# Transformer block on one core: SyncE's first 24 loads paced, and gate_m computed with the other modulation rows on TensorE

## Chip, core and metric

One core of one Trainium2 chip. The time is the device time in microseconds (us) of one execution. Engines: TensorE (PE; its weight loads are PEld), VectorE (DVE), ScalarE (ACT), GpSimd (POOL), and SyncE (SP), which only issues DMAs here.

## What is computed

A diffusion transformer block with adaptive modulation. B = 2, N = 256 tokens, D = 1152, two heads of 576, F = 4608, all inputs bf16.

```python
mod = (_silu(c) @ w_mod).reshape(B, 6, 1, D)
shift_a, scale_a, gate_a, shift_m, scale_m, gate_m = [mod[:, i] for i in range(6)]
h = _layernorm(x) * (1 + scale_a) + shift_a
q, k, v = split(h @ wqkv)
attn = _softmax(q @ k.T * Dh ** -0.5)
x = x + gate_a * ((attn @ v) @ wo)
h2 = _layernorm(x) * (1 + scale_m) + shift_m
return x + gate_m * (_gelu(h2 @ w_fc1) @ w_fc2)
```

The modulation vectors come from a product of two rows (one for each batch) with a 1152 x 6912 weight, so each of the six takes a 2.65 MB weight for two rows of result.

## The kernel before

**Tiling.** All 512 tokens are worked on at once. D is cut into 9 slices of 128 (`kt`), F into 36 (`f`, `j`). All weights pass once through one SBUF arena of 212,000 bytes per partition, whose regions (O_A, O_B, O_C, O_R, O_X and others) are used again by later stages. A reuse makes a DMA or an operation wait for the last reader.

**Stages on TensorE, in order.** Warm-up matmuls; transposes of the normalized x (`xn_T`); scale_a from three loads of w_mod for the first five slices (`mod_kt(WSC...)`, two columns per matmul); the K projection, slice by slice (`k_pair`), with the rest of scale_a in between; shift_a; the Q projection; scores and softmax; the V projection (`v_proj`), with the transposes of the softmax in between; after `v_proj(2, 0)` the modulation rows (`rows`); after `v_proj(3, 0)` their transposition into columns (`rows_T`); attention times V; the Wo projection (`wo_tile`) with gate_a, residual and second layernorm; fc1 with gelu; fc2 with gate_m, residual and store.

**The modulation rows.** `rows` (L964) computes gate_a, shift_m and scale_m as rows: the stationary operand is the two columns of silu(c) for a slice (`ST[:, kt:18:9]`), the moving one a piece of w_mod, and four matmuls lie side by side in the four 32-column groups of the array (`tile_position=(0, 32 * j)`). Pieces are 448 columns wide (`RW`), two for each group, so the 3456 columns take 18 groups of four over the nine slices, in PSUM banks 3 and 4. One ScalarE and one VectorE copy evict them to ROWS. GpSimd stores gate_a's row to a DRAM scratch and reads it back broadcast over all partitions (`gate_load(0, GA)`); the Wo stage multiplies by it at L1062. `rows_T` (L984) turns shift_m and scale_m into columns with 18 small matmuls.

**gate_m.** It is not among the rows. Its weight (WGM) is loaded by a DMA of its own after the V projection. `gate_m_sums` (L994) computes on VectorE, during fc1, the product by f32 multiply-adds: for each batch nine passes over 128 x 1152 (L1001 and L1004), with silu(c) as a scalar for each partition. Two 32x32 block transposes (L1008) and a reduction (L1010) fold the partitions in each block; `gate_m_rows` (L1012) sums over the four blocks with one small fp32 matmul on TensorE (GMS with QS), and goes over the same DRAM scratch to GM. ST32 and QS are prepared near the start (L726, L728).

**Loads.** SyncE issues all loads, in the order of the code: x in two halves; scale_a weights for the first five slices (three loads of 480 KB); K weights of slices 0 to 4 (288 KB each); the rest of scale_a (three of 384 KB); K weights of slices 5 to 8; shift_a (three of 864 KB); Q weights by slice; V; three of WMODR (2592 KB each); Wo; fc1 weights 0 to 3; WGM; fc2 weights; and further fc1 weights as their buffers come free. Up to shift_a no load waits for anything. The Q weights wait for TensorE to be done with the first matrix in that region.

**What sets the order.** `Sched` collects every operation with its reads and writes and works out dependences (`_track`). TensorE and SyncE keep the order of the code; VectorE and ScalarE follow a hand-written list at the start (`S.first`), and otherwise a list planner that uses estimated durations and the longest path behind each operation (`schedule`). `emit` turns dependences into semaphore waits. An explicit order puts gate_m's multiply-adds behind the eviction of the last `h2T` slices (L1186 to L1190).

Of the kernel before, what the change touches and what calls it, by code (L numbers as in the profile page):

```python
# [516 lines left out]
def c_mm(n):  # L517
    return max(n / 2.4 + 2.5, 27.0)
# [26 lines left out]
def build_kernel(nc, x, c, wqkv, wo, w_mod, w_fc1, w_fc2, out):  # L545
# [5 lines left out]
    with (  # L551
# [46 lines left out]
        WV = wmat(O_C, D)  # L598
        WMODR = wmat(O_R, 3 * D)
        WGM = wmat(O_R + 3 * W1, D)  # L600
        GMT = sb(O_R + 3 * W1, 9216, F32)
        WFC2 = sb(O_R, 4 * W1).rearrange("p (k f) -> p k f", k=JT)
# [14 lines left out]
        GM = [sb(o + 18432, 2304) for o in (O_A, O_C)]  # L617
        XN2 = [sb(O_R + 3 * W1 - (i + 1) * 2304, 2304) for i in range(4)]
        ROWS = sb(O_R + 3 * W1 - 5 * 2304, 1792)
        GMA = sb(O_X, 9216, F32)  # L620
        T1 = [sb(O_X + i * 1536, 1536, F32) for i in range(3)]
# [25 lines left out]
        NHALF = sb(misc(4), 4, F32)  # L647
        ST32 = sb(misc(72), 72, F32)
        GMS = sb(misc(288), 288, F32)
        QS = sb(misc(128), 128, F32)  # L650
        GMO = sb(misc(64), 64)
        MX = sb(misc(32), 32, F32).rearrange("p (i j) -> p i j", i=4)
# [27 lines left out]
        def copy_on(eng, dst, src, n, psum16, name):  # L680
            if eng == "act":
                act(c_act(n), lambda e: e.activation(out=dst, in_=src, func=ACTF.Copy), [src], [dst], name)  # L682
            else:
                dve(c_dve_psum16(n) if psum16 else c_dve_psum32(n), lambda e: e.tensor_copy(dst, src), [src], [dst], name)  # L684

        def mm(o, l, r, st, sp, **kw):
            S.instr(lambda e: e.matmul(o, lhsT=l, rhs=r, start=st, stop=sp, **kw), reads=[l, r], writes=[o])  # L687
# [36 lines left out]
        dve(170, lambda e: e.tensor_scalar(out=HC, in0=CT_PS, scalar1=0.5, scalar2=None, op0=ALU.mult), [CT_PS], [HC], "c_half")  # L724
        i3 = IDENT.rearrange("p (a i) -> p i a", a=4)
        dve(200, lambda e: e.tensor_reduce(out=QS, in_=i3, axis=AX.X, op=ALU.add), [IDENT], [QS], "qs")  # L726
        dve(170, lambda e: e.scalar_tensor_tensor(out=ST, in0=TH, scalar=1.0, in1=HC, op0=ALU.add, op1=ALU.mult), [TH, HC], [ST], "c_silu")
        dve(100, lambda e: e.tensor_copy(ST32, ST), [ST], [ST32], "st32")  # L728

# [231 lines left out]

        RW = 448
# [21 lines left out]
        def rows_T():  # L984
            S.unit("pe", 2 * KT * 27.0, "rowsT")
            for i in range(2 * KT):
                j, o = (KT + i) // 7, (KT + i) % 7
                mm(ps32(5, i * 2, 2), ROWS[0:98, o * 128:(o + 1) * 128], IDENT[0:98, 32 * j:32 * j + 2], i == 0, i == 2 * KT - 1,
                   skip_group_check=True)
            a, b_ = ps32(5, 0, 18), ps32(5, 18, 18)  # L990
# [3 lines left out]
        def gate_m_sums():  # L994
            wfc2_load(2)
            for b in range(2):
                acc = GMA[:, b * D:(b + 1) * D]
                for kt in range(KT):
                    w, s = WGM[:, kt, :], ST32[:, b * KT + kt:b * KT + kt + 1]
                    if kt == 0:  # L1000
                        dve(760, lambda e, w=w, s=s, acc=acc: e.tensor_scalar(out=acc, in0=w, scalar1=s, scalar2=None, op0=ALU.mult),  # L1001
                            [w, s], [acc], "gm_%d_%d" % (b, kt))
                    else:
                        dve(1270, lambda e, w=w, s=s, acc=acc: e.scalar_tensor_tensor(out=acc, in0=w, scalar=s, in1=acc, op0=ALU.mult, op1=ALU.add),  # L1004
                            [w, s, acc], [acc], "gm_%d_%d" % (b, kt))
            for b in range(2):
                acc, t = GMA[:, b * D:(b + 1) * D], GMT[:, b * D:(b + 1) * D]
                dve(1270, lambda e, acc=acc, t=t: e.transpose(t, acc), [acc], [t], "gm_tr%d" % b)  # L1008
            t, o = GMT.rearrange("p (c i) -> p c i", i=32), GMS
            dve(2500, lambda e: e.tensor_reduce(out=o, in_=t, axis=AX.X, op=ALU.add), [t], [o], "gm_sum")  # L1010

        def gate_m_rows():  # L1012
            S.unit("pe", 120.0, "gm_T")
            p = ps32(6, 0, 32)[0:72, :]
            mm(p, GMS, QS, True, True)
            dve(160, lambda e: e.tensor_copy(GMO[0:72, :], p), [p], [GMO[0:72, :]], "gm_ev")  # L1016
            dma(scratch[1].rearrange("b (c i) -> (b c) i", i=32), GMO[0:72, :], 2 * D * 2, "st_gm", eng="pool")
            gate_load(1, GM)

# [134 lines left out]
        for f in range(F0 - 2, F0):  # L1154
            fc1_tile(f, 0, 256)
        gate_m_sums()
        for f in range(F0):
            fc1_tile(f, 256, 256)
        for f in range(F0, JT):
            if f % 4 == 0 and f // 4 >= 4:  # L1160
                wfc1_load(f // 4)
            if f == 30:
                gate_m_rows()
            if f == 32:
                wfc2_load(3)
            fc1_tile(f, 0, 512)
# [18 lines left out]

        by = {u.name: u for u in S.units}  # L1186
        for u in S.units:
            if u.eng == "dve" and u.name.startswith("h2T_3"):
                S.order_after(by["gm_0_0"], u)
        S.order_after(by["gm_1_0"], by["gm_0_8"])  # L1190
        S.schedule()
# [52 lines left out]
```

## Time and profile before

| | |
|---|---|
| Median of 3 runs (lowest, highest) | 248.41 us (247.8, 248.61) |
| Profiled execution: time, span | 247.8 us, 246.1 us |
| TensorE busy | 240.2 us (98%) |
| VectorE busy | 99.2 us (40%) |
| ScalarE, GpSimd busy | 63.8 us, 20.2 us |
| Moved by DMA | 51.59 MB, mean 210 GB/s |
| Modulation weights for rows (L668, three loads of 2592 KB): issued, time to landing | 33.4, 35.0, 35.7 us; 15.2, 19.9, 26.9 us |
| Multiply-adds of gate_m (L1004) | 16 of 1416 ns, from 111.1 to 136.2 us |

How to read it: the span runs from the first to the last instruction of the program, and the time has 1.7 us around it. Busy times overlap between engines. A line number is that of the kernel before. Matmuls are issued before the one ahead has ended, so the time that one matmul costs in a row of them is the distance between starts, not its own duration. DMAs are shown by their issue and the time to their landing; the issuing instruction can be long over by then.

### The profile page before, as it was taken

The numbers are of one execution on the slowest core, as the hardware profiler recorded it, in microseconds if no ns is written. First come the engines' busy times: TensorE is split into PE (matmuls) and PEld (weight loads), VectorE is DVE, ScalarE is ACT, GpSimd is POOL, SyncE is SP. The second block draws the span as 40 slices with busy tenths as digits, with TensorE's granted clock in tenths as the row PEclk, the third lists the DMA queues.
The fourth block names the chain that finished last, engine by engine and source line by source line (L and its number), as shares of the span: only waits on it lengthen the run. The fifth ranks groups of instructions, "written<-read, shape, count | busy, mean of one in ns | idle before, by whom it ended". The sixth has DMA issues, their size and how long they took to land.

```text
span 246.1 us, 4095 instructions
## 1 busy us (share of the span) xinstructions
PE 240.2 (98%) x1789; PEld 149.3 (61%) x1789; DVE 99.2 (40%) x202; ACT 63.8 (26%) x129; POOL 20.2 (8%) x34
## 2 busy tenths in 40 slices
PE   6899999999999999999999999999999999999995
PEld 2589954557666766798544444444566666666675
DVE  2843440456312679969999700000011222211112
ACT  4830340344311405984322223322000000000000
POOL 1300000000011166500000000020000000000000
PEclk9999999999999999999999999999999999999999
DMA  6999989999993999969943579011000000000000
GB/s 232 362 377 392 390 307 410 420 421 409 389 349 91 332 381 392 390 228 394 352 121 131 189 246 377 3 30 67 0 19 16 16 19 17 16 16 19 24 24 19
DMA packets 28844, 51.59 MB, mean 210 GB/s; under 512 B 1559, under 2 KB 15643, under 8 KB 28827
## 3 DMA queue, kind: packets, MB, share of 16 engines
q1 hardware_dynamic: 28384, 50.14, 56.7%
q0 software_dynamic: 416, 1.19, 1.7%
q8 instruction: 14, 0.23, 0.4%
q14 instruction: 3, 0.02, 0.0%
q10 hardware_dynamic: 27, 0.00, 0.0%
HBM read 50.14 MB, written 1.19 MB: 209 GB/s over the span
## 4 chain that ended last, share of the span: by engine, by line
PE 93%; DMA 3%; ACT 1%; SPq 1%; DVE 0%; issue 0%
PE psum L687 91%; DMA arena<-in_w_mod_dram 3%; PE psum L690 2%; ACT arena L1084 1%; SPq L668 1%; ACT arena L1068 1%; DVE arena L795 0%; DVE arena L1182 0%; DVE arena L1183 0%; DVE arena L786 0%
## 5 line engine op out<-in xcount | busy, mean ns | idle before, releaser
L687 PE MATMUL psum<-arena 128*128 128x384 bf16 (+8 forms) x1700 | 236.5, 304 | 2.3 <-POOL arena L710 1.4
L687 PEld LDWEIGHTS psum<-arena 128*128 128x128 bf16 (+2 forms) x1700 | 144.0, 97 | 90.4 <-issue 3.2
L1182 DVE TENSOR_TENSOR arena<-psum,arena 128x384 f32<-128x384 f32 (+3 forms) x14 | 7.0, 500 | 68.0 <-PE psum L687 68.0
L1094 ACT ACTIVATE arena<-psum 128x512 bf16<-128x512 f32 (+1 forms) x44 | 22.5, 522 | 42.7 <-PE psum L687 42.7
L684 DVE CAST arena<-psum 128x512 bf16<-128x512 f32 (+4 forms) x22 | 13.6, 627 | 31.2 <-PE psum L687 31.0
L682 ACT ACTIVATE arena<-psum 128x512 bf16<-128x512 f32 (+7 forms) x29 | 15.5, 555 | 35.1 <-PE psum L687 32.6
L1004 DVE SCALAR_TENSOR_TENSOR arena<-arena 128x1152 f32<-128x1152 bf16 x16 | 22.7, 1416 | 0.5
L1063 POOL TENSOR_TENSOR arena<-arena 128x384 f32<-128x384 f32 x12 | 10.9, 911 | 13.3 <-DVE arena L1062 12.1
L668 POOL DMA_DIRECT2D dit_scratch<-arena x3 | 1.8, 610 | 116.4 <-ACT arena L682 59.6
L734 DVE BATCH_NORM_STATS2 arena<-arena 128x6 f32<-128x384 f32 (+1 forms) x18 | 9.5, 548 | 1.2 <-DMA arena<-in_x_dram 1.1
L1016 DVE CAST arena<-psum 72x32 bf16<-72x32 f32 x1 | 0.2, 187 | 21.2 <-PE psum L687 21.2
L690 PE MATMUL psum<-arena 128*128 128x128 bf16 (+1 forms) x89 | 7.3, 219 | 1.0 <-DMA arena<-in_c_dram 0.6
L690 PEld LDWEIGHTS psum<-arena 128*128 128x128 bf16 (+1 forms) x89 | 5.9, 98 | 3.5 <-DMA arena<-in_c_dram 1.5
L1068 ACT ACTIVATE arena<-arena 128x1152 bf16<-128x1152 f32 x4 | 5.4, 1354 | 9.5 <-DVE arena L1067 9.5
L1062 DVE TENSOR_TENSOR arena<-psum,arena 128x384 f32<-128x384 f32 x12 | 6.6, 548 | 3.2 <-PE psum L687 3.2
L1183 DVE TENSOR_TENSOR arena<-arena 128x384 bf16<-128x384 f32 (+3 forms) x14 | 7.0, 501 | 0.5
L1084 ACT ACTIVATE arena<-psum,arena 128x128 bf16<-128x128 bf16 x16 | 6.1, 460 | 3.2 <-PE psum L690 2.5
L1081 DVE TENSOR_SCALAR arena<-psum,arena 128x128 bf16<-128x128 bf16 x20 | 5.5, 337 | 1.9 <-PE psum L690 1.8
L934 ACT ACTIVATE arena<-psum,arena 128x256 bf16<-128x256 f32 x8 | 3.7, 470 | 6.9 <-PE psum L687 5.4
L738 POOL TENSOR_TENSOR arena<-arena 128x1 f32<-128x1 f32 x6 | 3.3, 552 | 9.0 <-DVE arena L737 9.0
L897 ACT ACTIVATE arena<-arena 128x256 bf16<-128x256 bf16 x6 | 2.5, 495 | 4.3 <-DVE arena L891 4.3
L795 DVE TENSOR_SCALAR arena<-psum,arena 128x256 bf16<-128x256 bf16 x7 | 2.4, 349 | 2.7 <-PE psum L690 1.4
(44 smaller groups left out, 43.9 us busy)
## 6 DMA issues: line engine op xcount, KB each, us to landing
arena<-in_w_mod_dram SPq DMA_DIRECT2D x4, 2592.0 KB, 19.1
arena<-in_w_fc_dram SPq DMA_DIRECT2D x9, 1152.0 KB, 8.1
arena<-in_w_fc_dram SPq DMA_DIRECT2D x4, 2592.0 KB, 16.5
arena<-in_wqkv_dram SPq DMA_DIRECT2D x18, 288.0 KB, 10.0
arena<-in_w_mod_dram SPq DMA_DIRECT2D x3, 864.0 KB, 12.2
arena<-in_wqkv_dram SPq DMA_DIRECT2D x1, 2592.0 KB, 9.3
arena<-in_wo_dram SPq DMA_DIRECT2D x1, 2592.0 KB, 33.1
arena<-in_w_mod_dram SPq DMA_DIRECT2D x3, 480.0 KB, 7.3
```

Of the source, the lines that this page charges most:

```text
L682: act(c_act(n), lambda e: e.activation(out=dst, in_=src, func=ACTF.Copy), [src], [dst], name)
L684: dve(c_dve_psum16(n) if psum16 else c_dve_psum32(n), lambda e: e.tensor_copy(dst, src), [src], [dst], name)
L687: S.instr(lambda e: e.matmul(o, lhsT=l, rhs=r, start=st, stop=sp, **kw), reads=[l, r], writes=[o])
L690: S.instr(lambda e: e.transpose(o, i_, idn), reads=[i_, idn], writes=[o])
L734: dve(550, lambda e, s=s, o=o: e.bn_stats(out=o, in_=s), [s], [o], "bn_%s_%d" % (tag, ci))
L1004: dve(1270, lambda e, w=w, s=s, acc=acc: e.scalar_tensor_tensor(out=acc, in0=w, scalar=s, in1=acc, op0=ALU.mult, op1=ALU.add), [w, s, acc] ...
L1063: S.op("pool", 930, lambda e, xs=xs, x1c=x1c: e.tensor_tensor(out=x1c, in0=x1c, in1=xs, op=ALU.add), reads=[x1c, xs], writes=[x1c], name=" ...
L1068: act(1344, lambda e: e.activation(out=xn2, in_=x1, func=ACTF.Identity, scale=rs, bias=nm), [x1, rs, nm], [xn2], "xn2_%d" % t)
L1084: act(440, lambda e, o=o, dst=dst, s1=s1, s2=s2: e.activation(out=dst, in_=o, func=ACTF.Identity, scale=s1, bias=s2), [o, s1, s2], [dst], ...
L1094: act(c_act(ntok), lambda e: e.activation(out=dst, in_=o, func=ACTF.Gelu_apprx_tanh), [o], [dst], "gelu_%d_%d" % (f, tok0))
L1182: dve(c_dve_psum32(w), lambda e, o=o, gm=gm, t1=t1: e.tensor_tensor(out=t1, in0=o, in1=gm, op=ALU.mult), [o, gm], [t1], "fc2_t1_%d_%d" % ( ...
L1183: dve(c_dve_32(w), lambda e, t1=t1, x1c=x1c, ost=ost: e.tensor_tensor(out=ost, in0=t1, in1=x1c, op=ALU.add), [t1, x1c], [ost], "fc2_out_%d ...
```

## The change

Two edits that do not depend on each other.

*Pacing.* `dma` keeps a list of the first 24 loads that SyncE issues (from x to the fourth Q weight). For each new one it walks back over the list, adds up the estimated bytes (real bytes times a factor from 1.0 to 1.42 for short runs), and where the sum goes over 1.2 MB it makes the new load depend on the landing of that load. SyncE then waits there, and everything behind it in its queue waits too.

*gate_m.* All VectorE work for it, its own weight load, its buffers and the small fp32 matmul go. WMODR becomes four matrices wide (three loads of 3456 KB), and `rows` computes all four vectors: the four column groups hold one vector each, in three pieces of 384 columns, so 27 groups of four, in PSUM banks 3, 4 and 5, with three evictions (VectorE, ScalarE, VectorE). The gate_m row is stored by GpSimd right behind that of gate_a. It is read back (`gate_load(1, GM)`) after the V projection. `rows_T` becomes 18 TensorE transposes, in banks 3 and 4. The normalized rows of the second layernorm (XN2) and ROWS move into the fourth quarter of WFC2's region. The first three quarters of fc2's weights are loaded in a row after the fc1 weights, and the fourth after the last `xn2_T`.

```diff
-        WMODR = wmat(O_R, 3 * D)
-        WGM = wmat(O_R + 3 * W1, D)
-        GMT = sb(O_R + 3 * W1, 9216, F32)
+        WMODR = wmat(O_R, 4 * D)
...
-        XN2 = [sb(O_R + 3 * W1 - (i + 1) * 2304, 2304) for i in range(4)]
-        ROWS = sb(O_R + 3 * W1 - 5 * 2304, 1792)
+        XN2 = [sb(O_R + 4 * W1 - (i + 1) * 2304, 2304) for i in range(4)]
+        ROWS = sb(O_R + 4 * W1 - 5 * 2304, 2304).rearrange("p (r c) -> p r c", r=3)
...
+        flight = []
+
         def dma(dst, src, nbytes, name, is_out=False, eng="sp", run=4096):
             eff = 1.0 if run >= 4096 else (1.08 if run >= 2304 else (1.15 if run >= 1536 else (1.3 if run >= 1024 else 1.42)))
-            return S.op(eng, 500.0 if eng == "sp" else 150.0, lambda e: e.dma_start(dst, src), reads=[src], writes=[dst],
-                        name=name, dma_bytes=nbytes * eff, is_out=is_out)
+            u = S.op(eng, 500.0 if eng == "sp" else 150.0, lambda e: e.dma_start(dst, src), reads=[src], writes=[dst],
+                     name=name, dma_bytes=nbytes * eff, is_out=is_out)
+            if eng == "sp" and not is_out and len(flight) < 24:
+                ahead = 0
+                for v in reversed(flight):
+                    ahead += v.dma_bytes
+                    if ahead > 1.2e6:
+                        u.instrs[0].deps.add(v.instrs[0])
+                        break
+                flight.append(u)
+            return u
...
-            dma(WMODR[:, k0:k0 + 3, :], wmod_v[:, k0:k0 + 3, 2 * D:5 * D], 3 * P * 3 * D * 2, "ld_modr%d" % k0)
+            dma(WMODR[:, k0:k0 + 3, :], wmod_v[:, k0:k0 + 3, 2 * D:6 * D], 3 * P * 4 * D * 2, "ld_modr%d" % k0)
...
+        row_banks = (3, 4, 5)
+        kind_base = (D, 2 * D, 3 * D, 0)
 
         def rows():
-            S.unit("pe", KT * 2 * c_mm(RW) + 100.0, "rows")
+            S.unit("pe", KT * 3 * c_mm(CH) + 200.0, "rows")
             for kt in range(KT):
-                for r in range(2):
+                for r in range(3):
                     for j in range(4):
-                        c0 = 2 * RW * j + RW * r
-                        n = min(RW, 3 * D - c0)
-                        bank = (3, 4)[r]
-                        mm(psum[32 * j:32 * j + 2, bank * 512:bank * 512 + n], ST[:, kt:18:9], WMODR[:, kt, c0:c0 + n],
-                           kt == 0, kt == KT - 1, tile_position=(0, 32 * j))
-            for r, eng in ((0, "act"), (1, "dve")):
-                copy_on(eng, ROWS[0:98, r * RW:(r + 1) * RW], ps32(3 + r, 0, RW)[0:98, :], RW, False, "rows_ev%d" % r)
-            dma(scratch[0, :, 0:2 * RW], ROWS[0:2, :], 2 * 2 * RW * 2, "st_ga0", eng="pool")
-            dma(scratch[0, :, 2 * RW:D], ROWS[32:34, 0:D - 2 * RW], 2 * (D - 2 * RW) * 2, "st_ga1", eng="pool")
+                        c0 = kind_base[j] + CH * r
+                        mm(psum[32 * j:32 * j + 2, row_banks[r] * 512: row_banks[r] * 512 + CH], ST[:, kt:18:9],
+                           WMODR[:, kt, c0:c0 + CH], kt == 0, kt == KT - 1, tile_position=(0, 32 * j))
+            for r in range(3):
+                copy_on("act" if r == 1 else "dve", ROWS[0:98, r, :], psum[0:98, row_banks[r] * 512: row_banks[r] * 512 + CH], CH, False, "rows_ev%d" % r)
+            for gi, j in ((0, 3), (1, 2)):
+                dma(scratch[gi], ROWS[32 * j:32 * j + 2, :, :].rearrange("p r c -> p (r c)"), 4608, "st_g%d" % gi, eng="pool")
             gate_load(0, GA)
...
         def rows_T():
-            S.unit("pe", 2 * KT * 27.0, "rowsT")
-            for i in range(2 * KT):
-                j, o = (KT + i) // 7, (KT + i) % 7
-                mm(ps32(5, i * 2, 2), ROWS[0:98, o * 128:(o + 1) * 128], IDENT[0:98, 32 * j:32 * j + 2], i == 0, i == 2 * KT - 1,
-                   skip_group_check=True)
+            for j, bank in ((0, 3), (1, 4)):
+                S.unit("pe", 9 * 30.0 + 100.0, "rowsT%d" % j)
+                for r in range(3):
+                    for i3 in range(3):
+                        ft = r * 3 + i3
+                        tr(ps16(bank, ft * 2, 2), ROWS[32 * j:32 * j + 2, r, i3 * 128:(i3 + 1) * 128], IDENT[32 * j:32 * j + 2, 32 * j:32 * j + 2])
...
         v_proj(3, 2)
+        gate_load(1, GM)
         wfc1_load(2)
         wfc1_load(3)
-
-        def wfc2_load(q4):
+        for q4 in range(3):
             dma(WFC2[:, 9 * q4:9 * q4 + 9, :], wfc2_v[:, 9 * q4:9 * q4 + 9, :], 9 * P * D * 2, "ld_wfc2_%d" % q4, run=2304)
-
-        dma(WGM, wmod_v[:, :, 5 * D:6 * D], D * D * 2, "ld_gm", run=2304)
-        wfc2_load(0)
-        wfc2_load(1)
...
-        gate_m_sums()
+        dma(WFC2[:, 27:36, :], wfc2_v[:, 27:36, :], 9 * P * D * 2, "ld_wfc2_3", run=2304)
...
-            if f == 30:
-                gate_m_rows()
-            if f == 32:
-                wfc2_load(3)
```

The functions `gate_m_sums` and `gate_m_rows`, the buffers ST32, GMS, QS and GMO, the operations that prepare QS and ST32, and the explicit order of the multiply-adds go too.

More of the change, by code (lines that the diff above doesn't have):

```diff
@@ L617, in build_kernel @@
         GM = [sb(o + 18432, 2304) for o in (O_A, O_C)]
-        XN2 = [sb(O_R + 3 * W1 - (i + 1) * 2304, 2304) for i in range(4)]
-        ROWS = sb(O_R + 3 * W1 - 5 * 2304, 1792)
-        GMA = sb(O_X, 9216, F32)
+        XN2 = [sb(O_R + 4 * W1 - (i + 1) * 2304, 2304) for i in range(4)]
+        ROWS = sb(O_R + 4 * W1 - 5 * 2304, 2304).rearrange("p (r c) -> p r c", r=3)
         T1 = [sb(O_X + i * 1536, 1536, F32) for i in range(3)]
@@ L647, in build_kernel @@
         NHALF = sb(misc(4), 4, F32)
[L648 to L651, printed above, removed]
         MX = sb(misc(32), 32, F32).rearrange("p (i j) -> p i j", i=4)
@@ L724, in build_kernel @@
         dve(170, lambda e: e.tensor_scalar(out=HC, in0=CT_PS, scalar1=0.5, scalar2=None, op0=ALU.mult), [CT_PS], [HC], "c_half")
-        i3 = IDENT.rearrange("p (a i) -> p i a", a=4)
-        dve(200, lambda e: e.tensor_reduce(out=QS, in_=i3, axis=AX.X, op=ALU.add), [IDENT], [QS], "qs")
         dve(170, lambda e: e.scalar_tensor_tensor(out=ST, in0=TH, scalar=1.0, in1=HC, op0=ALU.add, op1=ALU.mult), [TH, HC], [ST], "c_silu")
-        dve(100, lambda e: e.tensor_copy(ST32, ST), [ST], [ST32], "st32")
         def ln_stats_dve(src, chunks, bn_t, mv_t, rstd_t, tag):
@@ L959, in v_proj @@
             copy_on("act" if v_rr[0] % 2 else "dve", V[:, t, ci * CH:(ci + 1) * CH], o, CH, False, "v_ev%d_%d" % (t, ci))
-        RW = 448
+        row_banks = (3, 4, 5)
+        kind_base = (D, 2 * D, 3 * D, 0)
         def rows():
-            S.unit("pe", KT * 2 * c_mm(RW) + 100.0, "rows")
+            S.unit("pe", KT * 3 * c_mm(CH) + 200.0, "rows")
             for kt in range(KT):
-                for r in range(2):
+                for r in range(3):
                     for j in range(4):
-                        c0 = 2 * RW * j + RW * r
-                        n = min(RW, 3 * D - c0)
-                        bank = (3, 4)[r]
-                        mm(psum[32 * j:32 * j + 2, bank * 512:bank * 512 + n], ST[:, kt:18:9], WMODR[:, kt, c0:c0 + n],
-                           kt == 0, kt == KT - 1, tile_position=(0, 32 * j))
-            for r, eng in ((0, "act"), (1, "dve")):
-                copy_on(eng, ROWS[0:98, r * RW:(r + 1) * RW], ps32(3 + r, 0, RW)[0:98, :], RW, False, "rows_ev%d" % r)
-            dma(scratch[0, :, 0:2 * RW], ROWS[0:2, :], 2 * 2 * RW * 2, "st_ga0", eng="pool")
-            dma(scratch[0, :, 2 * RW:D], ROWS[32:34, 0:D - 2 * RW], 2 * (D - 2 * RW) * 2, "st_ga1", eng="pool")
+                        c0 = kind_base[j] + CH * r
[5 more added lines that the diff above has]
+                dma(scratch[gi], ROWS[32 * j:32 * j + 2, :, :].rearrange("p r c -> p (r c)"), 4608, "st_g%d" % gi, eng="pool")
             gate_load(0, GA)
@@ L984, in rows_T @@
         def rows_T():
-            S.unit("pe", 2 * KT * 27.0, "rowsT")
-            for i in range(2 * KT):
-                j, o = (KT + i) // 7, (KT + i) % 7
-                mm(ps32(5, i * 2, 2), ROWS[0:98, o * 128:(o + 1) * 128], IDENT[0:98, 32 * j:32 * j + 2], i == 0, i == 2 * KT - 1,
-                   skip_group_check=True)
-            a, b_ = ps32(5, 0, 18), ps32(5, 18, 18)
+            for j, bank in ((0, 3), (1, 4)):
[4 more added lines that the diff above has]
+                        tr(ps16(bank, ft * 2, 2), ROWS[32 * j:32 * j + 2, r, i3 * 128:(i3 + 1) * 128], IDENT[32 * j:32 * j + 2, 32 * j:32 * j + 2])
@@ L991, in rows_T @@
+            a, b_ = ps16(3, 0, 18), ps16(4, 0, 18)
             dve(170, lambda e: e.tensor_copy(SHM, a), [a], [SHM], "shm")
             dve(170, lambda e: e.tensor_scalar(out=SC1M, in0=b_, scalar1=1.0, scalar2=None, op0=ALU.add), [b_], [SC1M], "sc1m")
[L994 to L1018, printed above, removed]
         PVB = [(0, 1, 2, 6, 7), (3, 4, 5, 0, 1)]
@@ L1184, in build_kernel @@
                 dma(outv[b, :, t % 2, c0:c1], ost, P * w * 2, "st_out_%d_%d" % (t, c0), is_out=True)
[L1186 to L1190, printed above, removed]
         S.schedule()
```

## Prediction

> **What bounds the kernel now.** I read the page's busy shares and clock first: TensorE is busy 98% of the span, at full clock in every slice.
>
> ```profile
> PE 240.2 (98%) x1789; PEld 149.3 (61%) x1789; DVE 99.2 (40%) x202; ACT 63.8 (26%) x129; POOL 20.2 (8%) x34
> ...
> PE   6899999999999999999999999999999999999995
> ...
> PE 93%; DMA 3%; ACT 1%; SPq 1%; DVE 0%; issue 0%
> ```
>
> The last line is the chain that ended last: almost only TensorE, and one DMA. The chain in order of time says where that DMA stands.
>
> ```profile
> 2.83 7.91 DMA arena<-in_w_mod_dram
> 10.74 0.05 issue
> 10.79 0.67 PE psum L687 x15
> 11.46 0.02 issue
> 11.48 0.18 DVE arena L786
> ...
> 12.10 1.92 PE psum L687 x16
> ...
> 15.89 44.58 PE psum L687 x394
> ...
> 108.74 134.88 PE psum L687 x848
> ```
>
> Up to 12.1 us the kernel waits for the third load of the scale weights, which lands at 10.74; from there 1.36 us of small work leads to the first K matmul at 12.10. The 394 matmuls from 15.89 hold 97,408 columns in 277 matmuls, 41.3 us at 384 columns per 0.163 us (worked out below), and 117 two-column ones, 3.1 us at 0.027 (15 of them span 0.54, the last 0.165): 44.4 of 44.58 us, so there are no holes. After 12.1 us the kernel is TensorE from end to end: a change counts only where it moves 12.1, adds or takes matmuls, or makes TensorE wait. The VectorE work is not on the chain:
>
> ```profile
> L1004 DVE SCALAR_TENSOR_TENSOR arena<-arena 128x1152 f32<-128x1152 bf16 x16 | 22.7, 1416 | 0.5
> ...
> L687 PE MATMUL psum<-arena 128*2 128x448 bf16 x63 | 3.6, 352 | 0.0
> L687 PE MATMUL psum<-arena 128*2 128x320 bf16 x9 | 2.7, 299 | 0.0
> ```
>
> The 22.7 us lie at 111 to 136 us, beside fc1, whose releases go through ScalarE. The last two lines are the modulation rows on TensorE: 18 groups of four matmuls, side by side.
>
> **What the skill says.** The Trainium skill, DMA: Bandwidth & Descriptors, section Anatomy of one DMA, puts a fixed cost of about 2.0 us on one DMA (it measured another issue path). The trace agrees: the fc1 load issued alone at 126.4 lands after 5.6 us, while two in a row land 3.1 us apart (52.9+19.8 and 60.0+15.8), so about 2.3 us (3.3 us of transfer taken) is fixed, and its first bytes move about 1 us after the issue. The same page, Queues, rings and completion order: each of 16 engines takes its descriptors in ring order. The trace agrees: loads land in issue order, K weights 0.75 us apart. So a load queued behind does not slow one ahead of it on the same engine. TensorE: Matmul & The Clock Gate, Part 3, says column tiles run together within about 4 ns each; the 18 groups in 3.6 us agree.
>
> **The change, part by part.**
>
> *Pacing.* The build's wait list for SyncE shows the waits really in the program: the second scale load waits for the second x load, the third for the first scale load, the first two K-weight loads for the second scale load, and so on to the fourth Q-weight load. Queued behind each wait are all later loads, and behind those TensorE. Landings before (issue plus time to landing): x1 1.2+5.2=6.4, scale loads 8.2, 9.5, 10.74, first K weight 3.7+7.9=11.6. With waits, 0.1 us from landing to issue (SyncE issues the last store 0.09 after VectorE's end at 244.13), 2.3 fixed, 1.3 of transfer for a scale load and 0.75 for a K load:
> - second scale load: issued 6.5, lands 6.5+2.3+1.3 = 10.1 (was 9.5);
> - third: issued 8.3 (after 8.2). By its own latency it would land at 8.3+3.6 = 11.9, right behind the second at 10.1+1.3 = 11.4; I take 11.5 (was 10.74);
> - first K load: issued 10.2; 10.2+3.05 = 13.25 by latency, 11.5+0.75 = 12.25 by the queue; I take 13.0 (was 11.6).
>
> The first K matmul needs the third scale load plus 1.36 us (12.9) and the K load (13.0): it starts at about 13.1, **+1.0 us**, all on the path. From below: 0, if the slowest DMA engine, which sets each landing, still has older bytes to move when the late descriptors come; the isolated 2.3 contains the spread among engines. Less than 0 is the last rival. From above: +1.9, if latency adds in full each time and a restarted engine is slow. After that TensorE takes its time and each later load has cover: the last second-half scale load lands at 18.4 before, some 1.2 us later after, 19.6, and is needed near 20.3; the shift weights (28.8, about 30) are needed above 31; the Q weights have several us.
>
> The waits also leave holes in the transfers: the second to fourth Q loads wait for the last shift load (about 30). By the same steps the last Q load lands near 37.8 instead of 24.6+10.9 = 35.5: the DMA stream is **2.3 us late** from there.
>
> *Rows.* WMODR loads carry 4/3 of the bytes. Before, the V weights land at 42.2 and the three modulation loads at 48.6, 54.9 and 62.6, while rows start on TensorE near 67.2. After: V 44.5; then 6.35 x 4/3 = 8.4 each: 52.9, 61.3, and the third 69.7 (8.4) to 71.5 (7.7 x 4/3 = 10.2). Rows would start at 67.2+1.0 = 68.2; only its last third needs the third load, 2.9 us in, at 71.1. A slack of 4.6 us is gone: between 0 and 0.5 us of stall here, I take **+0.2**.
>
> TensorE's rows: 18 groups at (3.6-0.35)/17 = 0.19 us = 3.4 become 27 groups of 384 columns. Nine ordinary 128x384 matmuls span 1.63 us with the last at 0.33, so 0.163 each: 4.4 us, **+1.0**. The 18 small matmuls of the rows' transposition stay 18 small ones: 0. The fp32 matmul pair of gate_m goes: 0.3 us busy, but pipelined; **-0.1**.
>
> *VectorE.* 18 multiply-adds, two transposes, the reduction and three small copies go: about 30 us of work, off the path: 0. The rows add an eviction: VectorE now does two in sequence, 0.56 us each, so the gate store starts about 0.6 us later relative to the rows. Store, then gate load: before, issue at 71.7, gate in place at 76.6+3.9 = 80.5; needed by the VectorE multiply at 84.46. After: rows end 1.0+0.2+1.0 = 2.2 later, eviction 0.6, a full DMA queue perhaps 1: 84.3 against 86.7 needed. Cost 0; without that cover it would be the difference. GpSimd now also issues the gate_m store and loads ahead of the residual additions; the last waits for the V projection (about 79+2) and each issue takes 0.57, done before 86. Cost 0.
>
> *Moved loads.* The separate 2.6 MB load goes, the fc2 weights go one place up, their last quarter leaves at about 109+2 instead of 142 us. fc2 starts near 180. The Wo load lands at 69.4+2.3+5.1 (three times 8.4-6.3 less what the third may save), about 77 to 79, needed at 83+2; the first fc1 weights about 82, needed above 102. Cost 0.
>
> **Sum:** 1.0+1.0-0.1+0.2 = 2.1 us. The profiled execution took 247.8 with a span of 246.1, so 248.2 of span and 249.9. It was the fastest of three; their median is 248.41. Half of that difference added gives **250.2**.
>
> **Rivals.**
> - *The waits are hidden.* The slowest engine stays busy, the start does not move; only rows count: +0.9, or 248.7 from the profiled execution, 249.3 from the median. For it: 3.05 MB had moved by 10.74 us where x and scale weights are 2.66, so some engines ran 0.4 MB ahead and may idle without harm. Against it: the K load is issued after 10, not at 3.7. Chance 0.17.
> - *The delay adds up.* Start +1.9, third modulation load late by 1.3 or more, perhaps TensorE's clock falls: it idles for most of 8.6 to 14 us, and the Clock Gate page, Part 1, halves the clock after an idle window of about 3.4 us (the trace before shows no such fall after the warm-up). 1.9+0.9+1.3 = 4.1, 252.2; with the clock 253. Chance 0.13.
> - *Other side: the flood itself slows the head.* From 1.8 to 3.5 us only 239 GB/s move, against 387 from 3.5 to 6. If fewer queued loads cure that, 1.7 x 148 GB/s = 0.25 MB or 0.65 us is won, and the 0.4 MB that ran ahead is 1.0 us more: -1.65+0.9 = -0.75, 247.0. It decides from a gain above 0.9 at the third scale load. Against it: engines move K packets because they are done with theirs. Chance 0.04, and 0.04 for half of it (no change).
>
> Forecast 0.62. What can be told from no change is about 0.3%, 0.75 us. Slower: 0.62+0.13+0.11 of the first rival = 0.86; same 0.06+0.04 = 0.10; faster 0.04. Range: from 248.6 (waits hidden) to 252.4 (delay adds up).
>
> **What would show it.** First K matmul at 13.1 instead of 12.1, with the third scale load landing about 11.5 and the first K load about 13.0; last Q load near 37.8; third modulation load at 70 to 71.5 with a hole in TensorE inside the rows below 0.5 us; rows of 4.4 us; no other hole. Wrong if the first K matmul comes before 12.4 or after 14, or if TensorE waits at the gates or at Wo.

## The result and the profile after

The changed kernel takes 260.02 us (median of 4 runs, 257.56 to 260.88), against 248.15 us for the kernel before (4 runs beside it, 247.80 to 248.61): a ratio of 1.0461, with a 95% interval of 1.0384 to 1.0538. The forecast was 250.2 with a range up to 252.4. The sign was right and the size was wrong by a factor of about six: +11.9 us where about 1.8 were forecast. The ratios, here and below, were worked out from the single executions and so differ a little from the quotient of the two medians; all figures leave out three executions, two of e7 and one of e10, that took over 1.5% longer than the fastest of their kernel.

The profiled execution took 257.56 us with a span of 255.5 us. The page of the changed kernel, its busy shares, its clock and the shares of the chain:

```profile
PE 243.7 (95%) x1823; PEld 150.6 (59%) x1823; DVE 69.9 (27%) x179; ACT 63.8 (25%) x129; POOL 19.6 (8%) x33
...
PE   6679999999987999999999999999999999999995
PEclk9959999999999999999999999999999999999999
...
PE 76%; DMA 20%; SPq 2%; ACT 1%; issue 0%; DVE 0%
```

VectorE lost the 29 us of multiply-adds, as meant. TensorE now has two thin places, slices 0 to 2 and slices 11 to 12 (counted from 0, 6.4 us each), and a slice, number 2, at half the clock for the most part. The chain went from 3% DMA to 20%. In order of time it reads:

```profile
1.23 4.62 DMA arena<-in_x_dram
5.86 4.33 DMA arena<-in_w_mod_dram
10.20 3.98 DMA arena<-in_wqkv_dram
...
14.31 3.57 PE psum L691 x16
...
20.61 15.67 PE psum L691 x210
...
36.33 4.32 DMA arena<-in_wqkv_dram
...
44.90 33.52 DMA arena<-in_w_mod_dram
78.47 6.13 PE psum L691 x63
...
118.23 134.79 PE psum L691 x846
```

The first line is the second half of x; the next two are loads that SyncE did not issue before the one in the line above had landed. The K projection starts at 14.31 instead of 12.10. Its first 16 matmuls take 3.57 us instead of 1.92, at half clock. Then a Q load is awaited, and last the third modulation load: issued at 44.90, landed at 78.42. TensorE goes on at 78.47, in the middle of the modulation rows, and what follows has no hole: 177.0 us later the span ends. The last block of fc1 and fc2 matmuls is as long as before (134.79 against 134.88 us). So all of the loss lies ahead of 78.47.

Starts of the same work on TensorE, after minus before: first K matmul +2.2; after the half-clock stretch +4.7; Q projection +4.9; behind the wait for the second Q load +5.4; first of the rows +5.4; behind the rows +9.4 (1.0 for their nine further groups and 3.0 of waiting). The span is 9.4 us longer: nothing is added later.

The transfers show where the delay is made. The two kernels in the same stretches; the last three columns are the granted TensorE clock, the share of the DMA engines' time and the rate. Before:

```profile
core 0: us, PE busy (x) PEld busy (x) DVE busy (x) ACT busy (x) POOL busy (x), PEclk, DMA share, GB/s
6.00:15.00 9.00, 7.83 (x102) 5.80 (x101) 6.83 (x22) 5.92 (x12) 2.45 (x4) 1.00 1.03 369
15.00:30.00 15.00, 15.00 (x170) 13.25 (x169) 5.48 (x18) 3.83 (x7) 0.00 (x0) 1.00 1.06 386
30.00:46.00 16.00, 16.00 (x148) 8.45 (x146) 3.37 (x15) 3.05 (x8) 0.00 (x0) 1.00 0.99 372
```

After:

```profile
6.00:15.00 9.00, 5.15 (x75) 3.49 (x74) 5.98 (x19) 5.33 (x10) 2.45 (x4) 0.87 0.82 248
15.00:30.00 15.00, 15.00 (x153) 12.60 (x152) 3.41 (x14) 1.45 (x3) 0.00 (x0) 0.85 0.87 271
30.00:46.00 16.00, 15.61 (x166) 10.21 (x164) 5.39 (x17) 5.37 (x11) 0.00 (x0) 1.00 0.86 294
46.00:70.00 24.00, 24.00 (x154) 14.37 (x153) 11.62 (x25) 8.81 (x25) 0.00 (x0) 1.00 1.03 419
```

From 6 to 46 us the rate is lower by 121, 115 and 78 GB/s, which is 9 x 121 + 15 x 115 + 16 x 78 thousand bytes, 4.06 MB, or about 10.8 us at the 377 GB/s that the kernel before has there. The landings say the same: the last Q load lands at 45.71 instead of 35.51, **10.2 us late**. From 46 us on, with no pacing, the rate is full again (419 GB/s; 402 before), but the delay stays. The third modulation load comes 10.2 us late for these holes and 5.7 us for its 4/3 bytes and those of the two ahead of it: 62.56 + 15.9 = 78.4. Before, the rows needed it at 69.4, so there was a slack of 6.9 us. Even a TensorE that is itself 6 us late by then (5.4 and the longer rows) waits 3.0. So the loss can be counted a second way, along the loads alone: 10.2 + 5.7 - 6.9 = 9.0, and 0.3 for the last third of the rows, which are longer, is again the 9.4. In this count the late start and the half clock have no price of their own; e3 tests that.

### The profile page after: what moved, and what is told of

Same layout as the page of the kernel before. It is cut to its first block, busy times and chain, and to the rows that moved or that the text cites. A ratio compares the mean times of both kernels' runs of the same rounds, so it can differ in the third digit from the quotient of the medians.

```text
span 255.5 us, 4140 instructions
## 1 busy us (share of the span) xinstructions
PE 243.7 (95%) x1823; PEld 150.6 (59%) x1823; DVE 69.9 (27%) x179; ACT 63.8 (25%) x129; POOL 19.6 (8%) x33
## 4 chain that ended last, share of the span: by engine, by line
PE 76%; DMA 20%; SPq 2%; ACT 1%; issue 0%; DVE 0%
PE psum L691 74%; DMA arena<-in_w_mod_dram 15%; DMA arena<-in_wqkv_dram 3%; DMA arena<-in_x_dram 2%; SPq L663 2%; PE psum L694 2%; ACT arena L1060 1%; ACT arena L1044 1%; DVE arena L1150 0%; DVE arena L1151 0%
## 5 line engine op out<-in xcount | busy, mean ns | idle before, releaser
L691 PE MATMUL psum<-arena 128*128 128x384 bf16 (+7 forms) x1716 | 239.1, 307 | 8.1 <-DMA arena<-in_w_mod_dram 4.6
L691 PEld LDWEIGHTS psum<-arena 128*128 128x128 bf16 (+1 forms) x1716 | 144.3, 98 | 98.1 <-DMA arena<-in_w_mod_dram 5.3
L694 PE MATMUL psum<-arena 128*128 128x128 bf16 (+2 forms) x107 | 8.3, 217 | 1.0 <-DMA arena<-in_c_dram 0.6
L694 PEld LDWEIGHTS psum<-arena 128*128 128x128 bf16 (+2 forms) x107 | 6.8, 101 | 4.0 <-DMA arena<-in_c_dram 1.5
L794 ACT ACTIVATE arena<-psum,arena 128x256 bf16<-128x256 bf16 x3 | 1.3, 472 | 9.7 <-PE psum L691 6.5
L931 DVE TENSOR_REDUCE arena<-psum 128x2 f32<-128x512 f32 x4 | 2.8, 690 | 1.5 <-PE psum L691 1.5
```

What stands on the lines that cost most here:

```text
L694: S.instr(lambda e: e.transpose(o, i_, idn), reads=[i_, idn], writes=[o])
```

## Theories before the experiments

- **Holes in the stream.** The pacing leaves too little in the queue, so DMA stands idle at nearly every wait, and the holes add up; the end of the program follows the third modulation load. The half clock is a consequence that costs 2.5 us at the start. The rows' bytes turn the delay into a wait.
- **Rival: the clock.** The late start lets TensorE's clock fall, and keeping it up would give 2.5 us back.
- **Rival: the rows.** The rows, their evictions and stores are the larger part, whatever the pacing.
- **Rival: waiting as such.** SyncE's waits and the late issue of later loads cost, whatever the bytes in flight.

## Experiments

All kernels compute the whole reference. Those with filler add warm-up matmuls into a PSUM bank that is overwritten later; these leave the results as they are.

**e1: the pacing alone**, put into the kernel before; gate_m stays on VectorE.

```diff
+            if eng == "sp" and not is_out and len(flight) < 24:
+                ahead = 0
+                for v in reversed(flight):
+                    ahead += v.dma_bytes
+                    if ahead > 1.2e6:
+                        u.instrs[0].deps.add(v.instrs[0])
...
```

> The kernel before with the pacing alone. Theory (the pacing's holes in the load stream are the loss, and the rows' larger load makes them bite): first K matmul near 14.3 us, a half-clock window of TensorE as in the changed kernel, +5.4 us by the time rows start (72.6); the third modulation load lands 10.2 us later than before, at about 72.8, before rows needs it (72.6+2.3), so no stall in rows: about 253 us, 5 slower than before. Rival (the larger modulation load in front of rows is the loss): within 1 us of before. Rival (the stall in rows belongs to the pacing alone): about 256.

Measured: 253.78 us (252.89 to 254.93), ratio 1.0197 (1.0145 to 1.0249), about +4.1 against the median of 249.67 beside it. The chain of e1:

```profile
14.57 3.57 PE psum L698 x16
...
35.62 4.49 DMA arena<-in_wqkv_dram
...
40.24 25.10 PE psum L698 x142
...
70.62 30.37 PE psum L698 x256
```

The late start, the half clock and the late Q load are there without any rows. The last Q load lands at 45.94, 10.4 us late, as in the changed kernel. But the third modulation load, with 3/4 of the bytes, lands at 72.36 and the rows do not wait: they lie inside the 256 matmuls of the last line, 30.37 us as before. The profiled span is 4.9 us longer: 2.5 for the start, 1.8 for the half clock, the rest a wait for a Q load near 40 us. The same holes cost half as much here, since the slack still takes up the delay of the modulation loads.

**e2: the rows alone**, the changed kernel without pacing.

```diff
-            if eng == "sp" and not is_out and len(flight) < 24:
+            if eng == "sp" and not is_out and len(flight) < 0:
```

> The changed kernel without the pacing. Theory: start at 12.1, third modulation load at 62.6+5.6 = 68.2 against a need near 70, no stall, rows 1.0 us longer: 248.15+0.9 = 249.0. Rival (the larger load is the loss): a stall in rows of 2 us or more, 251 and up.

Measured: 250.27 us (22 runs, 248.60 to 252.26), ratio 1.0028 (1.0004 to 1.0052). The third modulation load lands at 69.97, and TensorE doesn't wait in the rows. So the rows are not the larger part. The two parts alone cost about 4.1 and 0.6 us and together 10 to 12: five to seven are an **interaction**. Of the 6.9 us of slack, the pacing alone leaves 1.9 (the third load is needed 4.9 us later than before, at 74.3, and lands at 72.36), and the rows' bytes take another 5.7. (In the profiled execution of e2 the third load lands 7.4 us later than before, 1.9 of it from the V load: that one was issued at 34.20, when only 1.1 us of loads was left in front of it. A queue that runs low makes a hole without pacing too.)

**e3 and e4: the clock kept up**, with 17 filler matmuls ahead of K, in the changed kernel (e3) and in e1 (e4).

```diff
         xn_T(0)
+        warm(3, "e")
...
+        warm(6, "c")
         for kt in range(6, 9):
...
         sc1a(0, KC)
+        warm(8, "d")
```

> The changed kernel with 17 idle-time matmuls on TensorE between the scale_a steps, so that its clock stays full. Theory (the changed kernel ends on the third modulation load at 78.4 us, whatever TensorE does before): the half-clock stretch goes, rows starts 2.5 us sooner and waits 2.5 us longer, time about as the fastest of the changed kernel (257.5), with less spread between runs. Rival (start, clock and stall add up on TensorE): 2.5 us less, 255 against 257.5.

> The kernel before with pacing and the same 17 idle-time matmuls. Theory: without the larger load there is no wait in rows or a short one, so the clock counts: 2.5 us less than with pacing alone, about 250.7, unless the third modulation load (72.8) is then late: rows would start near 70 and need it at 72.4, a stall of 0.4. Rival (the clock is not the cause of the 2.5 us between the first K matmul and the fourth slice): same as with pacing alone.

Measured: e3 258.17 us (256.08 to 259.84), ratio 1.0367 (1.0307 to 1.0427); e4 255.10 us (253.52 to 255.75), 1.0241 (1.0180 to 1.0301), no faster than e1. Clock and chain of e3:

```profile
PEclk9999976999999999999999999999999999999999
```

```profile
30.63 6.83 DMA arena<-in_w_mod_dram
...
37.50 4.33 PE psum L691 x35
...
46.03 33.04 DMA arena<-in_w_mod_dram
...
79.11 6.13 PE psum L691 x63
```

The filler does what it should: the clock is full when K starts. But TensorE then comes sooner to the shift weights and waits 3.5 us for the last of them, up to 37.50, and in that idle stretch the clock falls after all (slices 5 and 6). The third modulation load comes at 79.11 whatever TensorE did ahead of it, and the span is 256.1. In e4 the same: 2.2 us of waiting for the last shift load, and half clock from 38.0 to 41.4. For e3 I had expected no gain. For e4 I had expected 2.5 us, 250.7, and that was wrong by 4.4. The clock is a part of the path only as long as it is what is latest; behind it stands the stream of loads, which e1 alone did not let me see, because a TensorE at half clock reached the shift weights after they had landed.

**e5 and e10: more bytes in flight.** The changed kernel with 2.4 MB (e5) and 1.8 MB (e10) in place of 1.2 MB.

```diff
-                    if ahead > 1.2e6:
+                    if ahead > 2.4e6:
```

> The changed kernel with twice the bytes allowed ahead (2.4 MB in place of 1.2). Theory (a load issued into a nearly empty queue takes 3.0 to 3.6 us beyond its transfer, and 1.2 MB are only some 3 us of transfer, so every wait leaves a hole; 2.4 MB cover it): no holes, third modulation load near 69 to 70, first K matmul near 12.1 to 12.5; about 250, as without pacing. Rival (waiting on SyncE costs in itself, through the waits and issues): half of the loss stays, 254 or more.

> The changed kernel with 1.8 MB allowed ahead. Theory (a hole opens where less than about 3 us of transfer is left in the queue when a wait ends): the estimated bytes of the scale loads are 1.3 times the real ones, so small holes of about 1 us stay at the start and none among the K, shift and Q loads: first K matmul 0.5 to 1 us later than with 2.4 MB, no stall in rows: 250.5 to 252. Rival (a loss in proportion to the number of waits): half way between 260 and 249.8, about 255.

Measured: e5 249.82 us (20 runs, 248.71 to 251.08), ratio 1.0028 (1.0003 to 1.0053), the same as without pacing (e2). e10 253.15 us (252.39 to 253.24), ratio 1.0166 (1.0116 to 1.0216), over the 250.5 to 252 that I expected: I had taken holes to be nearly gone at 1.8 MB, and they are not, and TensorE waits 1.3 us in the rows, where I had expected no wait. Two of SyncE's waits in e5, with total, number and longest in us, and a piece of its chain:

```profile
SPq L663 <- DMA arena<-in_w_mod_dram: 5.8, 5, 2.2
SPq L663 <- DMA arena<-in_wqkv_dram: 4.1, 5, 1.9
```

```profile
17.53 44.59 PE psum L691 x394
```

With its two other kinds SyncE waits 16.6 us for landings in e5, at no cost: the 394 matmuls run without a hole, and the last Q load lands at 35.45 (35.51 before). So waiting as such is refuted. The number of waits hardly changes, 15, 13 and 14 with 1.2, 1.8 and 2.4 MB (26.9, 21.1 and 16.6 us in all), while the cost goes from 10 us to nothing. With 1.8 MB the last Q load lands at 40.33 and the third modulation load at 73.39; with 1.2 MB at 45.71 and 78.42. The chain of e10:

```profile
39.70 33.69 DMA arena<-in_w_mod_dram
...
73.44 6.13 PE psum L691 x63
```

73.44 + 177.0 gives 250.4, its span. The time follows the bytes in flight through that landing. The landings show where holes are left at 1.8 MB: four loads (the first and the last K load, the last shift load, the fourth Q load) land 0.9 to 2.1 us later than the load ahead of them plus their own transfer, and each was issued with 0.9 to 1.3 MB left in front of it. In e5 SyncE never waited until less than 1.5 MB was left, and no load behind a wait lands more than 0.1 us late by this count, except one (0.9), which the unpaced e9 shows too (0.8).

**e6 and e7: pacing of the first ten loads alone, or of the others alone.**

```diff
-            if eng == "sp" and not is_out and len(flight) < 24:
+            if eng == "sp" and not is_out and len(flight) < 10:
```

```diff
-                    if ahead > 1.2e6:
+                    if ahead > 1.2e6 and len(flight) >= 10:
```

> The changed kernel with only the first 10 loads paced (to the fifth K weight). Theory: first K matmul at 14.3 and a stretch at half clock, +4.7 us; fifth K weight 2.7 us late, later loads without holes, third modulation load near 71 to 72 and rows start near 72: no stall; about 253.5. Rival (start and clock cost nothing in the changed kernel's sum, the tail alone counts): 250.

> The changed kernel with only loads 11 to 24 paced. Theory: start as before (12.1), holes of some 7.5 us, last shift load near 33.6 with a wait of TensorE of 2 us there, third modulation load near 75.7; the end follows that load: about 254.5 to 255, more than with the head paced although TensorE starts on time. Rival (the late start is the main cost): about 251.

Measured: e6 253.69 us (252.34 to 254.06), ratio 1.0186 (1.0131 to 1.0242); e7 253.72 us (253.53 to 255.68), ratio 1.0193 (1.0119 to 1.0268). The profiled execution of e7 is the slowest of its three. In e6 K starts at 14.46 and the clock is half up to 19.1, and the last Q load is 4.4 us late; but the third modulation load, at 73.61, comes in time for the rows. In e7 K starts at 11.86, and the chain shows two waits:

```profile
26.53 6.78 DMA arena<-in_w_mod_dram
33.36 5.61 PE psum L691 x41
...
42.89 33.79 DMA arena<-in_w_mod_dram
76.73 6.13 PE psum L691 x63
```

2.2 us for the last shift load, with half clock from 34.6 to 38.0, and 3.0 in the rows; 76.73 + 177.0 = 253.7, its span. So, by the ratios and beside e2, each part of the pacing costs some 4 us of its own, the first through the start and the clock, the second through the landing of the third load.

**e8: the changed kernel again**, unchanged, on the chip of e5 to e7.

> The changed kernel as it is, for the same chip as the three others: 257.5 to 261, third modulation load at 78 to 79 us, rows stalled by 1 to 3.5 us depending on how long TensorE ran at half clock before.

Measured: 260.03 us (259.48 to 260.83), ratio 1.0453 (1.0397 to 1.0509). Its profiled execution is slower than that of the changed kernel shown above, 258.8 us of span. Its clock and chain:

```profile
PEclk9959999999997999999999999999999999999999
```

```profile
46.85 33.23 DMA arena<-in_w_mod_dram
...
80.13 7.76 PE psum L691 x63
```

The third load lands 1.7 us later than there, and right behind the wait in the rows the clock is half for 3.4 us, which makes the 63 matmuls 1.6 us longer. That landing, at 80.09, and the stall of 4.0 us both lie outside what I had expected of this run. So the 9.4 us worked out above belong to an execution that was the fastest of four; in others the stall also costs clock, and the median of +11.9 contains that. It contains some 1.5 us of the baseline too: the four executions of the kernel before beside it (247.80 to 248.61) all lie in the range of the faster of the two groups that e9 shows. Against the median of 23 executions on its own chip, 249.65, e8 is 10.4 us slower.

**e11: the rows later**, behind `v_proj(2, 2)`, with `rows_T` behind `v_proj(3, 2)`, in the changed kernel.

```diff
+        v_proj(2, 1)
+        v_proj(2, 2)
...
-        v_proj(2, 1)
-        v_proj(2, 2)
...
-        rows_T()
...
+        rows_T()
```

> The changed kernel with rows two V-projection units later (2.9 us of TensorE work that does not need the modulation load), and its transposition after the last V unit. Theory (TensorE waits in rows for the third modulation load): the wait of 3 us falls to nearly nothing, up to 2.9 us less, about 257; less gain if the gates, which come no sooner, become the next wait. Rival (the wait is only where TensorE happens to stand, the end is set elsewhere): same as the changed kernel, 260.

Measured: 257.43 us (255.15 to 258.78), ratio 1.0302 (1.0242 to 1.0362), 2.6 us less than e8 on another chip; the intervals of the two ratios don't overlap. The wait in the rows was a real cost and not a name for something else. The profiled execution was the slowest of the four, and in it the third load still comes too late (TensorE waits 2.3 us; 4.0 in e8):

```profile
80.46 7.74 PE psum L691 x45
...
104.54 0.54 DVE arena L1038
```

The last line is new on the chain: the multiplication by gate_a, which waited 3.0 us for the gate's rows from the DRAM scratch. So the cover that the prediction named for the gates was thin: in the changed kernel the first gate lands at 93.3 us, 0.6 before its first use, and in e2 at 86.56, 0.25 before it.

**e9 and e12: filler where the kernel before has a thin place.** The executions of the kernel before, and of e2 and e5, fall into two groups some 1.7 us apart. Those of the upper group have a mean clock of 0.992 to 0.993 (three of 0.986 lie still higher), and the profiled execution of e2, which is one of them, shows a window of half clock from 11.7 to 15.1 us. Six filler matmuls in the kernel before (e9), and the same in e2 (e12).

```diff
-        warm(14, "b")
+        warm(16, "b")
...
+        warm(1, "c")
         for kt in range(6, 9):
...
         sc1a(0, KC)
+        warm(3, "d")
```

> The kernel before with six more idle-time matmuls on TensorE ahead of the first K matmul (two more in the warm-up, one before and three after the last scale_a step). Theory (part of the spread of the kernel before, 247.5 to 251.2, is a half-clock window that some executions get at the first K matmuls because TensorE idled before): fewer such windows, median 0.5 to 1.5 us lower. Rival (the spread has another cause): same as before.

> The changed kernel without pacing and with the six idle-time matmuls ahead of the first K matmul. Theory: with a full clock in nearly all runs the rows' own price is left, 0.9 us over the kernel before with the same six matmuls (248.19): 249.1. Rival (the rows cost nothing): 248.2.

Measured: e9 248.19 us (22 runs, 247.92 to 249.98) against 249.26 (27 runs, 247.62 to 250.35) for the kernel before on the same chip, ratio 0.9980 (0.9961 to 0.9999). The window shows in 3 of 22 runs of e9 and in 15 of 27 of the kernel before. e12 249.16 us (14 runs, 248.58 to 250.56), ratio 0.9992 (0.9970 to 1.0014), one run of 14 with the window. Between executions at full clock e12 is about 1.0 us above e9 (medians 249.16 and 248.17, on two chips) and 0.95 above the kernel before on its own chip (248.21): that is the price of the rows on TensorE, forecast at +0.9. e9 is perhaps 0.2% faster than the kernel before, with an interval that all but touches 1. What it gains comes from the clock: between executions at full clock alone there is no gain (medians 248.17 for e9 and 247.98 for the kernel before).

## Why the prediction was wrong

**The start, +1.0 us forecast, +2.2 measured.** The step "Landings ... With waits, 0.1 us from landing to issue ..., 2.3 fixed" failed in its fixed part. The second scale load landed at 10.18 (forecast 10.1), but only because it was issued 0.6 us sooner than I had it, at 5.86: x landed at 5.84, and SyncE needed 0.02 us, not 0.1. From issue to landing it took 4.3 us for 1.3 of transfer, so 3.0 and not 2.3. The first K load took 3.98, less 0.75 of transfer, 3.2; the second Q load 4.32, so 3.6. My 2.3 came from one load of fc1, issued alone late in the program, and from 3.3 us of transfer; with the 3.1 us shown beside it, it would have been 2.5. (That x landed at 5.84 is not the change's doing: it landed at 5.6 to 6.0 in every other profile, at 5.83 in e2 without any pacing, and 6.46 is the odd one of the profile of before. Nor would the first load of the program have told the truth: from issue to landing it took 4.3 us before, 2.9 beyond its 1.4 of transfer, but 3.4 to 3.7 in every other profile, about 2.2 beyond it.) The bound from above (+1.9, "latency adds in full each time and a restarted engine is slow") was nearest and still too low, and I gave the rival built on it 0.13. The Trainium skill, DMA: Bandwidth & Descriptors, section Anatomy of one DMA — SWDGE (gpsimd) path, has about 2.0 us for another issue path; here the measured 3.0 to 3.6 decides.

**"After that TensorE takes its time and each later load has cover", 0 forecast: the step that failed most.** I priced a hole at the start and one at the Q loads and took the waits between them to be covered by the bytes still queued. The walk counts the awaited load itself, and estimated bytes that are 1.3 times the real ones for the scale loads and 1.08 times for the K, shift and Q loads. When a wait ends, what is left in the queue is 0.5 to 1.0 MB, 1.3 to 2.6 us of transfer, and once only one K-sized load of 0.75 us, while the new loads named above took 3.0 to 3.6 us on top of their own transfer, and the second shift load (issued 27.38, landed 34.13) even 4.4. So eight of the 15 waits end in a hole: the load behind them lands 0.5 to 2.3 us later than the load ahead of it plus its own transfer at 377 GB/s. SyncE's waits in the changed kernel (total, number, longest):

```profile
SPq L663 <- DMA arena<-in_w_mod_dram: 9.0, 6, 2.1
SPq L663 <- DMA arena<-in_wqkv_dram: 8.3, 6, 4.2
SPq L474 <- DMA arena<-in_w_mod_dram: 5.9, 2, 4.2
SPq L663 <- DMA arena<-in_x_dram: 3.7, 1, 3.7
```

15 waits, 26.9 us in all; I had priced two holes, one at the start and one at the Q loads. The delay of landings grows from one to the next: first K load +2.6 us, last first-half K load +2.7, last of the later scale loads +3.3, last K load +5.9, last shift load +7.4, last Q load +10.2. I had the last shift load at about 30 (36.27 measured) and the last Q load at 37.8 (45.71). e5 has 16.6 us of waits with more bytes behind each: no hole and no cost.

**The rows' stall, +0.2 forecast, 3.0 measured.** The method held, slack against delay, and so did the 8.4 us for each load (8.4, 8.9 and 8.7 measured). The delay put into it was 2.3 instead of 10.2 us. That the two parts of the change share one slack was in the prediction ("A slack of 4.6 us is gone"), and e1, e2 and e8 show it.

**The clock, left out of the forecast, 2.5 us measured.** I had it inside a rival only. The Trainium skill, TensorE: Matmul & The Clock Gate, Part 1, gives half clock after an idle window of about 3.4 us, and the trace agrees on the length: the stretches at half clock were 3.4 or 6.8 us. But it does not take a window that is idle throughout, so my own reason against the fall, that the trace before shows none, was weak. The clock records of the profiles change in steps of 3.41 us. In the last such window ahead of the fall at the start (9.26 to 12.68 in the changed kernel), the profile has TensorE busy for 1.5 of 3.41 us; over all profiles the clock fell at the start behind windows with up to 2.34 us of busy time (e2), and not behind those with 2.49 and more (2.55 in the kernel before). Where the windows begin differs from execution to execution. e3 shows that this cost could not be won back alone.

**What held.** The rows, +1.0 for nine further groups of 0.163 us (e12 against e9: about 1.0 net). VectorE's work off the path: 0. The fp32 pair gone, the transposes equal: within 0.1. Wo and fc1 loads: no wait. The gates: no wait, but by luck. I had given them 2.4 us of cover; the gate loads then took 6.2 us and more instead of 3.9, and 0.6 us was left (0.25 in e2). The rival "the waits are hidden" fell with e1. "The flood itself slows the head" shows nowhere: x lands as early in runs whose first loads are not paced (5.83 in e2, 5.73 in e7), and with them paced K starts late (14.46 in e6). "The delay adds up" had the mechanism, and with 252 to 253 a third of its size.

**Left open.** Why a load into a nearly empty queue takes 3.0 to 3.6 us beyond its transfer in this stretch and 2.3 in fc1 was not settled; no run took such a load alone. It is not fixed by the place either: the second Q load, 3.6 us here and 3.2 to 3.7 in e1, e7, e8 and e11, took 2.0 in e3 and e4. And why a stall in the rows sometimes costs clock fits the windows (busy for 1.2 us in the one ahead of the fall in e8 and e11, for 1.6 and more where none followed), but no run moved a window to test that.

## What to carry to other kernels

A limit on the bytes in flight has to leave, at the moment a wait ends, more transfer in the queue than a new load's own latency: count what is left behind the awaited load and in real bytes (with 1.5 MB and more there were no holes here; those that there were lay at 1.3 MB and less), and take the latency from several loads of the same stretch, the longest of them, since one alone misled here. A hole in a stream of loads is not made up while the stream is the bound (10.2 us at 45.71, and the same 10.2 in the landing at 78.42), so follow the sum of the holes to the next load that has little slack, and add up everything that draws on that slack before calling it cover. Before winning back a stall on one engine, look for what would be late next: here a full clock only moved the wait to a load.

## Not expected of the hardware

- From the landing of a load to the issue of one that waits for it, SyncE took 0.02 us (5.84 to 5.86, 10.18 to 10.20).
- The kernel before has a window of 3.4 us at half clock in 15 of 27 executions on one chip, going by their mean clock, and each costs 1.7 us; six small matmuls in a thin stretch lower that to 3 of 22 (e9).
- A stall of TensorE in the rows halved the clock for 3.41 us when it was 4.0 us (e8) and 2.3 us long (e11), and did not when it was 2.8 us long (the changed kernel and e7; the lengths are TensorE's idle time in the profile). In e8 that made the 63 matmuls behind it 1.6 us longer.
